# Smaller pieces in the loads, one copy on ScalarE, the mask on another queue, and warm-up matmuls behind the scores

## The chip, the cores and the metric

The kernel runs on one core of a Trainium2 chip. The metric is the time of one execution on the device in microseconds; lower is better.

## The reference

Two layers follow one another. The first is an attention over 8 batches, 8 heads, 576 positions and 64 numbers a head. Its output is the sum of a pooled attention (queries, keys and values averaged over groups of 4) and a local one, in which a position sees those less than 4 away. The second is a mixture of 8 experts: each of the 4,608 tokens goes to the expert with the largest logit, through two matrices with a ReLU between them, and the result is multiplied by the gate's probability.

```python
q_d = q.reshape(B, H, Sd, 4, D).mean(axis=3)      # k_d and v_d alike
out_up = np.repeat(sm_attn(q_d, k_d, v_d), 4, axis=2)
mask = np.abs(pos[:, None] - pos[None, :]) < 4
out_local = softmax(where(mask, scale * q @ k.T, -1e9)) @ v
x = (out_up + out_local)                          # as [4608, 512]
expert = argmax(x @ w_gate, axis=1)
y = probs[expert] * (relu(x @ w1[expert]) @ w2[expert])
```

## The kernel before

**Attention.** 32 passes each take two heads, which lie on the two halves of the 128 partitions. The list `PASS` writes out by hand in which order the steps of a pass are issued; a pair (step, lag) means that in pass i the step works for pass i - lag, so that steps of several passes are interleaved. `s_loc` computes the local scores in 10 blocks of 58 queries and 64 keys: four matmuls first add the mask, 40 more the products. `max_loc`, `sub_loc`, `exp_loc`, `sums`, `eps`, `inv` and `norm` make the softmax on VectorE and ScalarE, `t_loc` and `e_loc` transpose it, and `pv_loc` multiplies it with the values. The pooled attention has the same steps (`s_d`, `max_d`, `exp_d`, `t_d`, `e_d`, `pv_d`); its averages are made by GpSimd in `pool_qk`, `pool_qk2`, `pool_v` and `pool_v2`. `out_d` and `add_up` sum both into `XT`, the input of the second layer.

**Loads.** All loads of a pass are issued on SyncE's queue: `load_qk` (a row of 580 query and 586 key numbers on each of 128 partitions, three buffers), `load_vd` (a row of 1,024 numbers on each of 72 partitions, two buffers), `load_vw` (two buffers) and, from pass 11 on, quarters of the first expert's weights. A load waits until the buffer that it writes is free, and those behind it on the queue wait with it. ScalarE's queue carries the constants at the start: `cb`, the mask and `cf`.

**Routing.** Every four passes 4 or 5 tiles of 128 tokens are complete. The steps `r_mm` to `r_last` compute their expert and their place in that expert's block; the running count per expert is `crun`, which begins as a copy of eight constants after pass 2. `x_rows` turns the tokens back into rows, and `scatter` writes them by an indirect DMA of GpSimd. The state of a routing step lies in the dictionary `RS`.

**Warm-up.** Before and between the first passes `warm` issues matmuls of 128x512 zeros that nobody reads: 9 at the start, then 5, 8 and 5 after passes 0, 1 and 2 (`WARM`).

**Experts.** From about 190 us on `s1`, `s2`, `split_w1` and `split_w2` work through the experts, with float32 split into a high and a low part.

Of the kernel before, what the change touches and what calls it, by code (L numbers as in the profile page):

```python
# [29 lines left out]
KPAD = (NG - 1) * QB + KW  # L30
R = 4
# [12 lines left out]
WARM = (9, 5, 8, 5)  # L44
# [46 lines left out]
def attention_moe_kernel(ctx: ExitStack, tc: tile.TileContext, qk, vw, vd, wg, w1, w2, cst, csb, out):  # L91
# [33 lines left out]
    nc.scalar.dma_start(maskb, csb[:, B_MASK:])  # L125
# [113 lines left out]
    def s_loc(i):  # L239
# [8 lines left out]
        for c in range(NC):  # L248
            for h, t in ((0, 0), (1, 1), (0, 1), (1, 0)):
# [3 lines left out]
                                 x[r, QPAD + g * QB:QPAD + g * QB + KW],  # L253
# [142 lines left out]
    def r_mm(m, tiles):  # L396
        c = tiles[0] * 128
        p = RS[m, "p"] = bank()
# [10 lines left out]
    def r_lg(m, tiles):  # L409
        lg = RS[m, "lg"] = rp.tile([128, 384], F32, name="over", bufs=1)  # L410
        w = 256 if len(tiles) == 4 else 384
        nc.scalar.activation(lg[:, :w], RS[m, "p"][:, :w], AF.Copy)

    def r_turn(m, tiles):
        lg = RS[m, "lg"]
        p = RS[m, "p"] = bank()
# [6 lines left out]
    def r_max(m, tiles):  # L423
        T = len(tiles)
        RS[m, "pl"] = RS[m, "p"][:, :T * 32].rearrange("p (t e) -> p t e", e=32)[:, :, :E]
        RS[m, "m"] = rp.tile([128, 5], F32, name="rm")
        nc.vector.tensor_reduce(RS[m, "m"][:, :T], RS[m, "pl"], axis=AX.X, op=OP.max)

    def r_sub(m, tiles):
        T = len(tiles)  # L430
        d = RS[m, "d"] = RS[m, "p"][:, 256:296].rearrange("p (t e) -> p t e", e=E)
        nc.vector.tensor_sub(d[:, :T], RS[m, "pl"], RS[m, "m"][:, :T, None].to_broadcast([128, T, E]))

    def r_exp(m, tiles):
# [639 lines left out]
```

## Time and profile before

| | |
|---|---|
| median of 3 runs | 647.17 us (645.33 to 647.36) |
| the profiled execution | 644.67 us, its span 642.9 us |
| TensorE, share of the span busy | 96% |
| VectorE | 55% |
| ScalarE | 53% |
| GpSimd | 35% |
| SyncE's DMA queue, share of 16 engines | 49.0% |

The shares are averages over two unlike stages: in the attention passes all engines are busy, in the experts' stage TensorE alone is full. The span runs from the first to the last instruction of the profiled execution; its time also holds the start and the end.

### The profile page before, as it was taken

What the parts mean: (1) busy time and instruction counts of PE and PEld (TensorE: products, weight loads), DVE (VectorE), ACT (ScalarE), POOL (GpSimd) and SP (SyncE); (2) the same over time, 40 slices, a digit from 0 to 9 for tenths busy, and PEclk for the clock granted to TensorE, in tenths of its full rate; (3) what the DMA queues carried; (4) which work ended last, traced back from release to release, by engine and by line L of the source; (5) the groups of instructions that cost most, each with busy time, mean ns of one, the idle gap of its engine ahead of it and who ended that gap; (6) DMA issues with size and microseconds to landing.
All of it is one profiled execution on the core that took longest, in us unless ns stands there. A gap on an engine that the chain in (4) does not pass through costs nothing.

```text
span 642.9 us, 15721 instructions
## 1 busy us (share of the span) xinstructions
PE 617.6 (96%) x6123; PEld 507.9 (79%) x6123; DVE 352.3 (55%) x691; ACT 343.3 (53%) x941; POOL 226.6 (35%) x348
## 2 busy tenths in 40 slices
PE   7899999999979899999999999999999999999994
PEld 4678887787768798888888888888888888888873
DVE  5999988888854573751571174175038166115020
ACT  4899999999964353543452263264235154223120
POOL 7877899999924311111111101101011111110111
PEclk9999999999989999999999999999999999999997
DMA  8998999999862794383274276258137537010001
GB/s 286 286 269 285 292 302 286 292 280 290 239 195 84 187 304 136 122 224 90 84 191 138 66 187 192 68 155 213 56 109 183 181 112 197 35 47 1 34 18 43
DMA packets 68612, 108.65 MB, mean 169 GB/s; under 512 B 15724, under 2 KB 39804, under 8 KB 68496
## 3 DMA queue, kind: packets, MB, share of 16 engines
q1 hardware_dynamic: 62080, 87.78, 49.0%
q0 software_dynamic: 5984, 19.01, 7.9%
q8 instruction: 66, 1.08, 0.8%
q14 instruction: 50, 0.41, 0.2%
q10 hardware_dynamic: 432, 0.37, 0.2%
HBM read 87.09 MB, written 23.67 MB: 172 GB/s over the span
## 4 chain that ended last, share of the span: by engine, by line
PE 68%; issue 10%; POOL 7%; DMA 5%; DVE 5%; ACT 2%; SPq 1%; POOLq 0%; another core or an unknown queue 0%; DVEq 0%; ACTq 0%
PE p L675 8%; PE p L674 8%; PE p L676 8%; PE p L690 7%; PE p L688 7%; PE p L689 7%; POOL xs L550 2%; DMA vd<-in_vd_dram 2%; PE pD L305 2%; POOL vdt L230 2%; PE pX L770 2%; PE pX L789 2%; PE pX L342 1%; PE pS L251 1%; PE pX L329 1%
## 5 line engine op out<-in xcount | busy, mean ns | idle before, releaser
L695 POOL DMA_INDIRECT out_dram<-y,tix x39 | 37.9, 971 | 213.3 <-ACT y L707 201.9
L674 PE MATMUL p<-xh,w1h 128*128 128x512 f32 (+1 forms) x288 | 106.4, 370 | 0.8 <-ACT xh L621 0.7
L675 PE MATMUL p<-xl,w1h 128*128 128x512 f32 (+1 forms) x288 | 105.7, 367 | 0.8 <-DVE xl L622 0.8
L676 PE MATMUL p<-xh,w1l 128*128 128x512 f32 (+1 forms) x288 | 105.5, 366 | 0.0
L688 PE MATMUL p<-w2h,hh 128*128 128x512 f32 x256 | 101.1, 395 | 0.0
L689 PE MATMUL p<-w2l,hh 128*128 128x512 f32 x256 | 99.8, 390 | 0.5 <-DVE w2l L664 0.5
L690 PE MATMUL p<-w2h,hl 128*128 128x512 f32 x256 | 99.9, 390 | 0.0
L679 DVE SCALAR_TENSOR_TENSOR hl<-p,hh 128x512 fp32r<-128x512 f32 (+1 forms) x72 | 45.5, 632 | 94.3 <-ACT hh L678 93.6
L678 ACT ACTIVATE hh<-p 128x512 fp32r<-128x512 f32 (+1 forms) x72 | 39.6, 551 | 78.1 <-PE p L676 75.6
L707 ACT ACTIVATE y<-p,gi 128x512 f32<-128x512 f32 x32 | 22.0, 689 | 91.2 <-PE p L690 86.8
L674 PEld LDWEIGHTS p<-xh,w1h 128*128 128x128 f32 x288 | 54.7, 190 | 10.7 <-ACT xh L621 1.1
L675 PEld LDWEIGHTS p<-xl,w1h 128*128 128x128 f32 x288 | 54.7, 190 | 9.6 <-DVE xl L622 0.9
L676 PEld LDWEIGHTS p<-xh,w1l 128*128 128x128 f32 x288 | 54.6, 190 | 8.7
L689 PEld LDWEIGHTS p<-w2l,hh 128*128 128x128 f32 x256 | 48.1, 188 | 10.6 <-DVE w2l L664 0.9
L690 PEld LDWEIGHTS p<-w2h,hl 128*128 128x128 f32 x256 | 48.1, 188 | 10.2
L688 PEld LDWEIGHTS p<-w2h,hh 128*128 128x128 f32 x256 | 48.1, 188 | 9.5
L664 DVE TENSOR_TENSOR w2l<-raw,w2h 128x512 fp32r<-128x512 f32 x64 | 43.3, 681 | 2.1 <-DMA xs<-xr,ix 1.5
L622 DVE TENSOR_TENSOR xl<-pX,xh 128x512 fp32r<-128x512 f32 x38 | 24.7, 684 | 35.2 <-ACT xh L621 34.2
L194 ACT ACTIVATE w1h<-raw 128x512 fp32r<-128x512 f32 (+1 forms) x72 | 42.1, 584 | 0.0
L550 POOL DMA_INDIRECT xs<-xr,ix x36 | 36.4, 1012 | 15.6 <-ACT xr L525 6.9
L663 ACT ACTIVATE w2h<-raw 128x512 fp32r<-128x512 f32 x64 | 39.8, 626 | 2.8 <-DMA xs<-xr,ix 2.8
L230 POOL TENSOR_TENSOR vdt<-vd 72x512 f32<-72x512 f32 x32 | 40.9, 1279 | 0.3
(152 smaller groups left out, 1240.1 us busy)
## 6 DMA issues: line engine op xcount, KB each, us to landing
raw<-in_w_dram SPq DMA_DIRECT2D x59, 512.0 KB
qk<-in_qk_dram SPq DMA_DIRECT2D x32, 583.0 KB
vw<-in_vw_dram SPq DMA_DIRECT2D x32, 320.0 KB
vd<-in_vd_dram SPq DMA_DIRECT2D x32, 288.0 KB
xrow<-xs SPq DMA_DIRECT2D x32, 192.0 KB
xrow<-xs SPq DMA_DIRECT2D x32, 128.0 KB
xs<-zs SPq DMA_DIRECT2D x6, 512.0 KB
raw<-in_w_dram SPq DMA_DIRECT2D x20, 128.0 KB
```

The source lines that it names most:

```text
L194: nc.scalar.activation(hi[:, s], src[:, s], AF.Copy)
L230: nc.gpsimd.tensor_add(t2, v[:, 0:2], v[:, 2:4])
L550: ins = nc.gpsimd.indirect_dma_start(out=xs, out_offset=bass.IndirectOffsetOnAxis(ap=IDX[m, t], axis=0), in_=xr, in_offset=None)
L663: nc.scalar.activation(hi, src, AF.Copy)
L664: nc.vector.tensor_sub(lo, src, hi)
L674: nc.tensor.matmul(p, wh[:, fs], xh[:, k, r], start=(k == 0), stop=False)
L675: nc.tensor.matmul(p, wh[:, fs], xl[:, k, r], start=False, stop=False)
L676: nc.tensor.matmul(p, wl[:, fs], xh[:, k, r], start=False, stop=(k == 3))
L679: nc.vector.scalar_tensor_tensor(hl[:, f, r], p, 0.0, hh[:, f, r], op0=OP.max, op1=OP.subtract)
L688: nc.tensor.matmul(p, hh, wh, start=(f == 0), stop=False)
L689: nc.tensor.matmul(p, hh, wl, start=False, stop=False)
L690: nc.tensor.matmul(p, hl, wh, start=False, stop=(f == 7))
```

## The change

- `load_qk` and `load_vd` keep their amount, but their rows land in several pieces with a gap of two numbers behind each: the row of queries and keys as two pieces of 586 numbers (six columns of padding are added to the queries), the row of pooled values as four of 256. The host lays the queries out accordingly, and `pool_qk`, `pool_v` and `s_loc` read at the new offsets.
- The mask is loaded on SyncE's queue, behind the first queries.
- The first copy of `crun` is issued on ScalarE instead of VectorE.
- Warm-up: 4 matmuls after pass 0; 7 in pass 2 and 5 in pass 3, each directly behind that pass's `s_loc`; none between passes 1 and 2.
- `RS` gets the first tile into its keys, and `x_rows`, `split_w2` and `s1` are cut into helper functions that are called in the order in which their instructions stood.

```diff
...
 PC = 2 * QB
 QPAD = NG * QB
 KPAD = (NG - 1) * QB + KW
+KOFF = KPAD + 2
 R = 4
 SD = S // R
 DB = 48
...
 NT = N // 128
 NX = 9
 NEG = -8.0e9
-WARM = (9, 5, 8, 5)
+WARM = (9, 4, 7, 5)
 
 C_ID, C_TOK, C_CAP, C_DESC, C_SUM = 0, 128, 164, 172, 180
 C_PAIR = C_SUM + 32
...
     QK, VW, VD, QKD, VDS, A, AD, AT, XT, MXD, SMD, ADT, PS_, PD, PV, IV, QKT, VDT, MX, BX, IVD = ({} for _ in range(21))
 
     def load_qk(i):
-        QK[i] = p1.tile([128, QPAD + KPAD], F32, name="qk", bufs=3)
-        nc.sync.dma_start(QK[i], qk[i])
+        QK[i] = p1.tile([128, 2 * KOFF], F32, name="qk", bufs=3)
+        nc.sync.dma_start(QK[i].rearrange("p (a x) -> p a x", a=2)[:, :, :KPAD], qk[i].rearrange("p (a x) -> p a x", a=2))
 
     load_qk(0)
     cb = consts.tile([128, B_MASK], BF, name="cb")
     nc.scalar.dma_start(cb, csb[:, :B_MASK])
     maskb = p1.tile([128, B_END - B_MASK], BF, name="mask", bufs=1)
-    nc.scalar.dma_start(maskb, csb[:, B_MASK:])
+    nc.sync.dma_start(maskb, csb[:, B_MASK:])
     load_qk(1)
     cf = consts.tile([128, C_END], F32, name="cf")
     nc.scalar.dma_start(cf[:, :C_LIM], cst[:, :C_LIM])
...
     nc.vector.memset(wsrc, 0.0)
     wp = psPV.tile([128, 1024], F32, name="pPV")[:, :512]
 
-    def warm(n, late=False):
-        p = bank() if late else wp
+    def warm(n):
         for _ in range(n):
-            nc.tensor.matmul(p, wsrc[:, :128], wsrc, start=True, stop=True)
+            nc.tensor.matmul(wp, wsrc[:, :128], wsrc, start=True, stop=True)
 
     warm(WARM[0])
     wgt = consts.tile([128, 4, 32], F32, name="wgt")
...
     nc.vector.memset(onesf, 1.0)
 
     def load_vd(i):
-        VD[i] = p1.tile([DC, R, 2, 2, D], F32, name="vd")
-        nc.sync.dma_start(VD[i].rearrange("p r c h d -> p (r c h d)"), vd[i])
+        VD[i] = p1.tile([DC, R, 4 * D + 2], F32, name="vd")
+        nc.sync.dma_start(VD[i][:, :, :4 * D], vd[i].rearrange("p (r x) -> p r x", r=R))
 
     def load_vw(i):
         VW[i] = p2.tile([128, NC, 2, D], F32, name="vw", bufs=2)
...
         x = QK[i]
 
         def sl(r):
-            return bass.AP(tensor=x.tensor, offset=x.offset + r, ap=[x.ap[0], [QPAD + HALO, 2], [R, SD], [2, 2]])
+            return bass.AP(tensor=x.tensor, offset=x.offset + r, ap=[x.ap[0], [KOFF + HALO, 2], [R, SD], [2, 2]])
         t1 = p1.tile([128, 2, SD, 2], F32, name="qkt", bufs=1)
         nc.gpsimd.tensor_add(t1, sl(0), sl(1))
         QKT[i] = t1
...
         nc.gpsimd.tensor_add(QKD[i], t1[:, :, :, 0], t1[:, :, :, 1])
 
     def pool_v(i):
-        v = VD[i]
+        v = VD[i][:, :, :4 * D].rearrange("p r (c h d) -> p r c h d", c=2, h=2)
         t2 = p1.tile([DC, 2, 2, 2, D], F32, name="vdt", bufs=1)
         nc.gpsimd.tensor_add(t2, v[:, 0:2], v[:, 2:4])
         VDT[i] = t2
...
                 g, s, r = 2 * c + t, h ^ t, slice(h * 64, h * 64 + 64)
                 nc.tensor.matmul(p[t * 64:t * 64 + QB, s * 512 + c * KW:s * 512 + (c + 1) * KW],
                                  x[r, g * QB:(g + 1) * QB],
-                                 x[r, QPAD + g * QB:QPAD + g * QB + KW],
+                                 x[r, KOFF + g * QB:KOFF + g * QB + KW],
                                  start=False, stop=(c == NC - 1), skip_group_check=True)
 
     def halves(a):
...
     def r_mm(m, tiles):
         c = tiles[0] * 128
-        p = RS[m, "p"] = bank()
+        p = RS[m, tiles[0], "p"] = bank()
...
-    def x_rows(m, t):
-        p = bank()
+    def x_tr(m, t):
+        p = BX["x", m, t] = bank()
         for k in range(4):
             nc.tensor.transpose(p[:, k * 128:(k + 1) * 128], XT[m][:, k, t * 128:(t + 1) * 128], ident)
+
+    def x_ev(m, t):
+        p = BX.pop(("x", m, t))
         xr = xrs[:, x_slot(m, t)]
         nc.scalar.activation(xr[:, :DM].rearrange("p (b k d) -> p k b d", k=4, d=32),
                              p.rearrange("p (k b d) -> p k b d", k=4, d=32), AF.Copy)
+
+    def x_rows(m, t):
+        x_tr(m, t)
+        x_ev(m, t)
 
     prev_sc = []
 
...
         nc.gpsimd.memset(t, 0.0)
 
     def split_w2(e, f):
+        w2_open(e, f)
+        w2_part(e, f, 0)
+        w2_part(e, f, 1)
+
+    def w2_open(e, f):
         if (e, f) == (0, 0):
             home("tgi", 2)
             home("ttix", 1)
             home("gap", 16)
-        hi, lo = W2[e, f] = tuple(mp[f // 6].tile([128, DM], F32R, name=f"w2{n}{f}") for n in "hl")
+        W2[e, f] = tuple(mp[f // 6].tile([128, DM], F32R, name=f"w2{n}{f}") for n in "hl")
+
+    def w2_part(e, f, n):
+        hi, lo = W2[e, f]
         src = raws[place[2, e, f // 2]][:, (f % 2) * 512:(f % 2) * 512 + 512]
-        nc.scalar.activation(hi, src, AF.Copy)
-        nc.vector.tensor_sub(lo, src, hi)
+        if n == 0:
+            nc.scalar.activation(hi, src, AF.Copy)
+        else:
+            nc.vector.tensor_sub(lo, src, hi)
+
+    HP = {}
 
     def s1(e, f, r=slice(0, FIRST)):
+        for n in range(3):
+            s1_part(e, f, r, n)
+
+    def s1_part(e, f, r, n):
         if e not in HT:
             HT[e] = tuple(mp[0].tile([128, 8, FIRST], F32R, name=f"h{w}") for w in "hl")
-        xh, xl = XH[e, 0]
-        p = h_bank()[:, :r.stop - r.start]
-        fs = slice(f * 128, (f + 1) * 128)
-        for k in range(4):
-            wh, wl = W1[e, k]
-            nc.tensor.matmul(p, wh[:, fs], xh[:, k, r], start=(k == 0), stop=False)
-            nc.tensor.matmul(p, wh[:, fs], xl[:, k, r], start=False, stop=False)
-            nc.tensor.matmul(p, wl[:, fs], xh[:, k, r], start=False, stop=(k == 3))
         hh, hl = HT[e]
-        nc.scalar.activation(hh[:, f, r], p, AF.Relu)
-        nc.vector.scalar_tensor_tensor(hl[:, f, r], p, 0.0, hh[:, f, r], op0=OP.max, op1=OP.subtract)
+        if n == 0:
+            xh, xl = XH[e, 0]
+            p = HP[e, f] = h_bank()[:, :r.stop - r.start]
+            fs = slice(f * 128, (f + 1) * 128)
+            for k in range(4):
+                wh, wl = W1[e, k]
+                nc.tensor.matmul(p, wh[:, fs], xh[:, k, r], start=(k == 0), stop=False)
+                nc.tensor.matmul(p, wh[:, fs], xl[:, k, r], start=False, stop=False)
+                nc.tensor.matmul(p, wl[:, fs], xh[:, k, r], start=False, stop=(k == 3))
+        elif n == 1:
+            nc.scalar.activation(hh[:, f, r], HP[e, f], AF.Relu)
+        else:
+            nc.vector.scalar_tensor_tensor(hl[:, f, r], HP.pop((e, f)), 0.0, hh[:, f, r], op0=OP.max, op1=OP.subtract)
 
     def down(e, hcol, get, between={}):
         p = get()
...
         if 11 <= i < 31:
             raw_part((i - 11) // 4, (i - 11) % 4)
 
+    def keep(i):
+        if 2 <= i < len(WARM):
+            warm(WARM[i])
+
     PASS = (
-        (exp_loc, 1), (rb_turn, 5), (t_d0, 3), (rc_place, 6), (eps, 2), (max_d, 1), (inv, 2), (s_loc, 0),
+        (exp_loc, 1), (rb_turn, 5), (t_d0, 3), (rc_place, 6), (eps, 2), (max_d, 1), (inv, 2), (s_loc, 0), (keep, 0),
         (rb_max, 5), (ld_qk, -2), (pool_qk, -1), (w1_hi, 0), (ld_vd, -1), (inv_d, 2), (rb_sub, 5), (ld_x, 0),
         (pv_loc, 3), (norm, 2), (rb_eps, 6), (e_d1, 3), (rb_top, 5), (rc_rk, 6), (max_scale, 1), (e_d0, 3),
         (max_loc, 0), (norm_d, 2), (ra_mm, 4), (pv_d, 3), (rb_first, 5), (rc_cs, 6), (rb_exp, 5), (pool_v2, 1),
...
     steps(-1)
     for i in range(NP):
         steps(i)
-        if i + 1 < len(WARM):
-            warm(WARM[i + 1], i >= 3)
+        if i == 0:
+            warm(WARM[1])
         if i == 2:
-            nc.vector.tensor_copy(crun, cf[:, C_CAP:C_CAP + E])
+            nc.scalar.copy(crun, cf[:, C_CAP:C_CAP + E])
         if i == 28:
             nc.sync.dma_start(cf[:, C_LIM:], cst[:, C_LIM:])
         if i == 29:
...
 
 
 def _layout(q, k, v):
-    qp = np.zeros((B, H, D, QPAD), q.dtype)
+    qp = np.zeros((B, H, D, KPAD), q.dtype)
     qp[..., :S] = q.transpose(0, 1, 3, 2)
     kp = np.zeros((B, H, D, KPAD), k.dtype)
     kp[..., HALO:HALO + S] = k.transpose(0, 1, 3, 2)
-    qk = np.concatenate([qp.reshape(NP, 128, QPAD), kp.reshape(NP, 128, KPAD)], axis=2)
+    qk = np.concatenate([qp.reshape(NP, 128, KPAD), kp.reshape(NP, 128, KPAD)], axis=2)
     vp = np.zeros((B, H, KPAD, D), v.dtype)
     vp[:, :, HALO:HALO + S] = v
     w = np.stack([vp[:, :, g * QB:g * QB + KW] for g in range(NG)], axis=2)
```

## Rows read from the trace of the kernel before

In the tables of stretches a row gives start and end (us), its length, then for TensorE, its weight loads, VectorE, ScalarE and GpSimd the busy time with the number of instructions, TensorE's granted clock, the DMA share and GB/s. In the orders of time a row gives start, length (us), engine, line, operation, what it writes and reads with shapes, and in brackets the idle time before it and what ended that.

**Rows 1.** Stretches of the attention passes.

```profile
20.00:46.00 26.00, 24.42 (x604) 19.45 (x605) 24.86 (x51) 23.91 (x91) 19.90 (x22) 1.00 0.96 276
46.00:57.00 11.00, 10.89 (x253) 9.28 (x253) 10.63 (x26) 11.00 (x46) 7.46 (x11) 1.00 0.84 246
57.00:110.00 53.00, 52.37 (x1243) 43.10 (x1243) 47.24 (x110) 51.17 (x189) 49.71 (x69) 1.00 0.98 295
```

**Rows 2.** The chain that ended last (start, length, work).

```profile
16.64 2.28 DVE crun L925
```

**Rows 3.** Order of time on VectorE, 14 to 26 us.

```profile
14.23 0.82 DVE L264 TENSOR_REDUCE mx<-pS 128x10 f32<-128x640 f32 x1 [0.44 <-PE pS L251]
...
16.56 2.37 DVE L925 COPY crun<-cf 128x8 f32<-128x8 f32 x1
...
18.84 0.59 DVE L310 TENSOR_REDUCE mxd<-pD 128x3 f32<-128x432 f32 x1
...
20.53 0.82 DVE L264 TENSOR_REDUCE mx<-pS 128x10 f32<-128x640 f32 x1
...
25.28 0.82 DVE L264 TENSOR_REDUCE mx<-pS 128x10 f32<-128x640 f32 x1
```

**Rows 4.** Order of time on GpSimd beside that copy.

```profile
17.75 1.14 POOL L219 TENSOR_TENSOR qkt<-qk 128x576 f32<-128x576 f32 x1
```

**Rows 5.** Order of time on ScalarE, 15 to 20 us.

```profile
15.95 0.74 ACT L271 ACTIVATE A<-A 128x640 f32<-128x640 f32 x1 [0.21 <-DVE A L268]
...
19.47 0.20 ACT L313 ACTIVATE mxd<-mxd 128x3 f32<-128x3 f32 x1 [2.22 <-DVE mxd L310]
```

**Rows 6.** Line 505: count, then min/median/max ns, first and last start.

```profile
L505 ACT COPY xr<-cf x8: 183/216/221, 50.7 to 201.2; 128x4 f32<-128x4 f32 x4, 128x5 f32<-128x5 f32 x4
```

**Rows 7.** Order of time on TensorE, 11 to 24 us.

```profile
11.44 1.90 PE L138 MATMUL pPV<-wsrc 128*128 128x512 bf16 x8
13.27 0.33 PE L245 MATMUL pS<-mask,cb 64*64 64x320 bf16 x4
...
16.43 1.24 PE L138 MATMUL pPV<-wsrc 128*128 128x512 bf16 x5
...
20.02 0.72 PE L370 MATMUL pPV<-ADT,vds 72*64 72x144 f32 x8 [0.65 <-ACT ADT L350]
...
22.11 0.95 PE L305 MATMUL pD<-qkd 64*64 64x144 f32 x12 [0.67 <-ACT AD L319]
...
23.69 0.33 PE L245 MATMUL pS<-mask,cb 64*64 64x320 bf16 x4
```

**Rows 8.** Waits up to 14 us (total, times, longest).

```profile
PE pS L245 <- DMA mask<-in_csb_dram: 1.0, 1, 1.0
```

**Rows 9.** Stretches with loads of 4,096, 2,048 and 512 B.

```profile
372.60:373.50 0.90, 0.90 (x6) 0.74 (x5) 0.90 (x3) 0.55 (x2) 0.00 (x0) 1.00 0.95 385
425.40:426.80 1.40, 1.40 (x8) 1.17 (x7) 0.57 (x2) 0.82 (x2) 0.00 (x0) 1.00 0.99 386
327.00:329.00 2.00, 2.00 (x10) 1.65 (x10) 1.35 (x3) 1.64 (x3) 0.00 (x0) 1.00 1.22 192
```

**Rows 10.** GpSimd's waits, 20 to 57 us (total us, times, longest).

```profile
POOL qkt L219 <- DMA qk<-in_qk_dram: 6.5, 5, 1.8
```

**Rows 11.** Order of time on SyncE's queue, two issues.

```profile
20.37 0.43 SPq L119 DMA_DIRECT2D qk<-in_qk_dram  x1
...
72.90 0.44 SPq L119 DMA_DIRECT2D qk<-in_qk_dram  x1
```

**Rows 12.** Order of time on GpSimd, the uses of these two loads.

```profile
26.39 1.15 POOL L219 TENSOR_TENSOR qkt<-qk 128x576 f32<-128x576 f32 x1 [1.28 <-DMA qk<-in_qk_dram]
...
80.79 1.15 POOL L219 TENSOR_TENSOR qkt<-qk 128x576 f32<-128x576 f32 x1
```

**Rows 13.** GpSimd's groups, 57 to 110 us (busy us, mean ns, idle).

```profile
L230 POOL TENSOR_TENSOR vdt<-vd 72x512 f32<-72x512 f32 x10 | 12.8, 1284 | 0.1
...
L219 POOL TENSOR_TENSOR qkt<-qk 128x576 f32<-128x576 f32 x9 | 10.3, 1148 | 0.0
```

More of the change, by code (lines that the diff above doesn't have):

```diff
@@ L409, in r_lg @@
     def r_lg(m, tiles):
-        lg = RS[m, "lg"] = rp.tile([128, 384], F32, name="over", bufs=1)
+        lg = RS[m, tiles[0], "lg"] = rp.tile([128, 384], F32, name="over", bufs=1)
         w = 256 if len(tiles) == 4 else 384
-        nc.scalar.activation(lg[:, :w], RS[m, "p"][:, :w], AF.Copy)
+        nc.scalar.activation(lg[:, :w], RS[m, tiles[0], "p"][:, :w], AF.Copy)
     def r_turn(m, tiles):
-        lg = RS[m, "lg"]
-        p = RS[m, "p"] = bank()
+        lg = RS[m, tiles[0], "lg"]
+        p = RS[m, tiles[0], "p"] = bank()
         for u in range(2):
@@ L447, in r_first @@
         T = len(tiles)
-        nc.vector.tensor_reduce(RS[m, "m"][:, :T], RS[m, "sc"][:, :T], axis=AX.X, op=OP.max)
+        nc.vector.tensor_reduce(RS[m, tiles[0], "m"][:, :T], RS[m, tiles[0], "sc"][:, :T], axis=AX.X, op=OP.max)
     def r_hot(m, tiles):
         T = len(tiles)
-        oh = RS[m, "oh"] = rp.tile([128, 5, E], BF, name="oh")
-        nc.vector.tensor_tensor(oh[:, :T], RS[m, "sc"][:, :T], RS[m, "m"][:, :T, None].to_broadcast([128, T, E]),
+        oh = RS[m, tiles[0], "oh"] = rp.tile([128, 5, E], BF, name="oh")
+        nc.vector.tensor_tensor(oh[:, :T], RS[m, tiles[0], "sc"][:, :T], RS[m, tiles[0], "m"][:, :T, None].to_broadcast([128, T, E]),
                                 op=OP.is_equal)
@@ L457, in r_gate @@
         T = len(tiles)
-        gt = RS[m, "gt"] = rp.tile([128, 5], F32, name="gt")
-        nc.vector.tensor_reduce(gt[:, :T], RS[m, "ex"][:, :T], axis=AX.X, op=OP.add)
+        gt = RS[m, tiles[0], "gt"] = rp.tile([128, 5], F32, name="gt")
+        nc.vector.tensor_reduce(gt[:, :T], RS[m, tiles[0], "ex"][:, :T], axis=AX.X, op=OP.add)
     def r_eps(m, tiles):
         T = len(tiles)
-        gt = RS[m, "gt"]
+        gt = RS[m, tiles[0], "gt"]
         nc.scalar.activation(gt[:, :T], gt[:, :T], AF.Copy, bias=1e-9)
@@ L477, in r_cs @@
     def r_cs(m, tiles):
-        cs = RS[m, "cs"] = rp.tile([128, E], F32, name="cs")
-        nc.vector.tensor_reduce(cs, RS[m, "oh"][:, :len(tiles)].rearrange("p t e -> p e t"), axis=AX.X, op=OP.add)
+        cs = RS[m, tiles[0], "cs"] = rp.tile([128, E], F32, name="cs")
+        nc.vector.tensor_reduce(cs, RS[m, tiles[0], "oh"][:, :len(tiles)].rearrange("p t e -> p e t"), axis=AX.X, op=OP.add)
     def r_run(m, tiles):
-        nc.gpsimd.tensor_add(crun, crun, RS[m, "cs"])
+        nc.gpsimd.tensor_add(crun, crun, RS[m, tiles[0], "cs"])
     def r_rk(m, tiles):
         T = len(tiles)
-        rk = RS[m, "rk"] = rp.tile([128, 5, E], F32, name="rk", bufs=1)
-        nc.vector.tensor_mul(rk[:, :T], RS[m, "p"][:, :T * E].rearrange("p (t e) -> p t e", e=E), RS[m, "oh"][:, :T])
+        rk = RS[m, tiles[0], "rk"] = rp.tile([128, 5, E], F32, name="rk", bufs=1)
+        nc.vector.tensor_mul(rk[:, :T], RS[m, tiles[0], "p"][:, :T * E].rearrange("p (t e) -> p t e", e=E), RS[m, tiles[0], "oh"][:, :T])
     def r_pos(m, tiles):
         T = len(tiles)
-        pos = RS[m, "pos"] = rp.tile([128, 5], F32, name="pos")
-        nc.vector.tensor_reduce(pos[:, :T], RS[m, "rk"][:, :T], axis=AX.X, op=OP.add)
+        pos = RS[m, tiles[0], "pos"] = rp.tile([128, 5], F32, name="pos")
+        nc.vector.tensor_reduce(pos[:, :T], RS[m, tiles[0], "rk"][:, :T], axis=AX.X, op=OP.add)
     def r_ix(m, tiles):
```

26 lines of the change are left out of this document (13 added, 13 removed).

## The prediction

> **What bounds the kernel now.** I read the table of stages first. From 20 to 110 us the kernel is in its attention passes, and there no engine alone is full: from 20 to 46 us VectorE works 24.86 of 26.00 us, from 57 to 110 us TensorE works 52.37 and GpSimd 49.71 of 53.00 us, and the DMA engines show a share of 0.96 and 0.98 in these two, and 0.84 in the eleven microseconds between [rows 1]. TensorE's granted clock is 1.00 throughout these stretches. Most of the change lies in the first four passes, so I read each engine's order of time there. In the chain that ended last the first copy of the count stands with 2.28 us, on VectorE [rows 2]. So in this stage a wait on VectorE is a delay of everything. Later the chain passes to ScalarE, GpSimd and TensorE, but each of these is reached through the one before it, in program order; a pass that starts earlier on VectorE starts earlier on all of them, as long as the loads come in time. That condition is where the prediction can fail.
>
> **The copy of the count.** The copy of 128x8 numbers takes 2.37 us on VectorE, from 16.56 to 18.93 us. The maximum over 128x640 numbers takes 0.82 us [rows 3], so the length of that row is not work. GpSimd runs an addition from 17.75 to 18.89 us, and the copy ends 0.04 us after that [rows 4]: it looks as if it waited for GpSimd to let go. Without it the next row, the pooled maximum at 18.84 us, starts 2.28 us earlier by the chain's piece, and that is the gain. ScalarE, which waited 2.22 us for that maximum, no longer does [rows 5]. On ScalarE the same kind of copy, 128x4 or 128x5 from the same tile, takes 0.183 to 0.221 us [rows 6]. It is issued between the last eviction of pass 2 and the exponential of pass 3, and there ScalarE is idle 0.21 us for VectorE [rows 5]: cost nothing, and 0.2 us where that gap closes. Behind it on ScalarE stand that exponential and what VectorE sums from it; the matmul that reads the count first is in the routing of pass 9.
>
> **The warm-up matmuls.** After pass 0 four run instead of five. Eight take 1.90 us [rows 7], so one is 0.24 us; the scores of pass 1 stand right behind them on TensorE, so up to 0.24 us comes back. In pass 2 eight stood in front of the scores, which start at 13.27 us; now seven stand behind them. The scores could start 1.8 us earlier, but VectorE is idle only 0.44 us for them before its maximum at 14.23 us [rows 3], so at most 0.44 us of this counts. In pass 3 five, 1.24 us, move from in front of the scores to in front of the local values' matmuls. The work up to the scores of pass 4 keeps its sum: from 16.43 to 23.69 us are 7.26 us, in which TensorE idles 0.65 and 0.67 us for ScalarE [rows 7], which now comes sooner. That leaves 5.94 us and puts the scores of pass 4 at 22.4 us, or at 22.0 us with 0.4 us of what was won before. From their start to the maximum that waits for them pass 2 shows 0.9 us (13.27 to 14.2 us), so they are ready at 22.9 us; VectorE took them up at 25.28 us [rows 3] and, 2.5 to 2.8 us ahead, wants them at 22.5 to 22.8 us. I take 0.5 us of gain from the warm-ups and 0.2 us of loss for this limit; the ends are a gain of 0.7 us and a loss of 0.4 us.
>
> **The mask's queue.** TensorE waits 1.0 us for the mask before the first scores [rows 8]. On the queries' queue it lands behind the first queries. Little of this counts, since the pooled scores, which come next on TensorE, need the queries that GpSimd pools meanwhile. In return the second queries and the first two blocks of values go behind 160 KB, some 0.6 us at the 276 GB/s of the first stretch [rows 1]. GpSimd waits for them, but its results are used passes later. I take nothing; the ends are a gain of 1.0 us, the whole wait, and a loss of 0.6 us.
>
> **The pieces.** A row of queries and keys becomes two pieces of 2,344 B instead of one of 4,664 B, a row of pooled values four of 1,024 B instead of one of 4,096 B. That is 128 and 216 packets more in a pass, 344 in all, 21.5 for each of 16 DMA engines. No row prices these sizes in this stage; I bound them by stretches of the expert stage in which one size is moved. With 4,096 B the rate is 385 GB/s at a share of 0.95, 405 GB/s for full engines; with 2,048 B it is 386 at 0.99, 390 GB/s [rows 9]. For one of 16 engines that is 162 ns for 4,096 B and 168 ns for two pieces: 6 ns for an added packet. With 512 B it is 192 at 1.22, 157 GB/s [rows 9], or 52 ns a piece where the rate of 2,048 B would give 21 ns: 31 ns for a packet. So a pass costs each DMA engine 0.13 us more at the one end and 0.67 us at the other; a gain I can't exclude either, since the new pieces also share the engines with others in another order. I take 0.15 us, near the row of 2,048 B, because 2,344 B is most of the bytes. Six columns of padding add 0.5% to a load, 0.01 us.
>
> The Trainium skill speaks against this edit: by "DMA: Bandwidth & Descriptors", in the section on why small descriptors are slow, a packet carries about three cycles over its 32-byte beats. At the beat of the 4,096 B rows (1.3 ns) that would be an estimate of 4 ns a packet, 0.08 us a pass instead of my 0.13 us; the trace agrees in direction, with 6 ns.
>
> Is it hidden? It is while queries land before GpSimd asks. From 20 to 57 us GpSimd waits for them five times, 6.5 us in all [rows 10], but with slack behind it. A load that was waited for took 6.0 us from issue to use (20.37 to 26.39 us); the shortest from 57 to 110 us is 7.9 us (72.90 to 80.79 us), and there GpSimd idles 0.0 us for them [rows 11 to 13]. So 1.9 us or less of cover is left, less because the DMA share is higher there. With 0.15 us a pass over the ten passes of that stretch 1.5 us is used up, and nothing is lost. The edits to the routing's keys and to the split helper functions issue the same instructions in the same order and cost nothing.
>
> **Sum.** 2.28 + 0.5 - 0.2 = 2.58 us of gain, say 2.5. The profiled execution took 644.67 us, 642.9 of them in the span; that becomes 642.2. The median of the runs is 647.17 us, 2.5 above the profiled execution, so I forecast 644.7. The runs lie up to 2.0 us apart; a change within 0.3% (1.94 us) can't be told from none.
>
> **Rivals.** *The DMA engines take the gain back.* If all passes come 2.5 us earlier, the same bytes have to land in less time. By the shares the DMA engines are idle 1.0 us of 20 to 46, 1.8 us of 46 to 57 and 1.1 us of 57 to 110 us [rows 1]: 3.9 us in all. For it speaks that GpSimd already waits for queries before 57 us; against it the 7.9 us above. If half of the idle time can't be filled, and the pieces take 1.5 us of the cover, the gain shrinks to about 0.6: 646.6 us.
>
> *The smaller pieces make the kernel slower.* From 20 to 110 us there are some eighteen passes (ten additions of values from 57 us on [rows 13], and eight before at 4.75 us each, the distance of the maxima at 20.53 and 25.28 us [rows 3]). At 31 ns a packet they cost 12.1 us of DMA time; 3.9 us of idle time and 1.9 us of cover take part of it, 6.3 us shows as GpSimd waiting for queries, less 2.5: 3.8 us slower, 651.0 us. It decides from (2.5 + 1.94 + 3.9 + 1.9) / 18 = 0.57 us a pass on, or 26 ns a packet. For it speaks the row of 512 B, against it that of 2,048 B.
>
> *GpSimd's addition of the values gets cheaper.* It takes 1.284 us for 72x512 numbers, while the addition of the queries takes 1.148 us for more, 128x576 [rows 13]. One difference is that the two operands of the former lie 2,048 B apart; with the two new columns they lie 2,064 B apart. At the rate of the other it would take 1.02 us, 0.26 us less in each of ten passes in which GpSimd has no idle time: 2.6 us on top, 642.1 us. Nothing shows that distance is the cause.
>
> **How the numbers follow.** The gain arrives (2.0 to 3.2 us): 0.40. With cheaper additions: 0.12. Taken back in part or whole (0 to 1.9 us): 0.31. Pieces slow the loads: 0.17, of which 0.14 by more than 0.3%. Hence faster 0.52, same 0.34, slower 0.14. The range goes from 641.0 (cheaper additions, and 1 us for the runs' spread) to 649.2, which leaves out the upper part of the slow case; the likeliest case alone has 643.9 to 645.2.
>
> **What would show it.** The maximum of pass 3 right behind the sums, no copy on VectorE, the scores of pass 4 near 22 us, and GpSimd's first scatter of routed rows earlier by 2.5 us. Waits of GpSimd for queries between 57 and 110 us would show the first two rivals, more than 6.5 us of them before 57 us the start of it; an addition of values near 1.0 us the third. I am wrong if VectorE finds another wait at 16 us, if TensorE's granted clock falls below 1.00 in one of these stretches, or if the 2.5 us are there at 46 us and gone at 110 us.

## The result and the profile of the changed kernel

The changed kernel took 655.5 us (median of 4 runs, 654.41 to 656.58) against 647.26 us (4 runs of the kernel before, 645.33 to 648.45): ratio 1.0132, 95% interval 1.0106 to 1.0158. The forecast was 644.7 us. The profiled execution took 654.67 us with a span of 652.9 us, 10.0 us more than before.

The stretches that answer to [rows 1], and the one ahead of them:

```profile
10.00:20.00 10.00, 7.53 (x125) 5.14 (x126) 6.83 (x11) 5.70 (x23) 8.98 (x10) 0.83 0.85 231
20.00:46.00 26.00, 23.15 (x568) 17.97 (x569) 20.91 (x42) 20.67 (x79) 19.61 (x22) 0.93 0.98 268
46.00:57.00 11.00, 9.63 (x216) 8.03 (x214) 10.36 (x29) 10.20 (x41) 6.70 (x10) 1.00 0.92 258
57.00:110.00 53.00, 51.48 (x1179) 42.59 (x1180) 44.38 (x102) 47.51 (x176) 43.91 (x61) 0.97 0.92 259
```

VectorE has lost 3.95 us of work between 20 and 46 us and GpSimd 5.8 us between 57 and 110 us, so these engines now stand still where they were the pace. The granted clock, 1.00 in all of [rows 1], is 0.93 and 0.97 in two of these stretches and 0.83 from 10 to 20 us. What stands still first is read from the waits. TensorE's, up to 110 us (total, times, longest):

```profile
PE pS L251 <- issue: 2.6, 1, 2.6
PE pPV L357 <- issue: 2.5, 1, 2.5
PE pD L305 <- POOL qkd L225: 1.9, 2, 1.3
...
PE pS L251 <- DMA qk<-in_qk_dram: 1.2, 2, 0.8
```

"Issue" is time in which the engine waited for nothing that the profile shows. In two places TensorE stands 2.5 us and more in the middle of a step. In order of time the first one reads:

```profile
27.35 0.72 PE L370 MATMUL pPV<-ADT,vds 72*64 72x144 f32 x8
...
30.44 0.72 PE L251 MATMUL pS<-qk 64*58 64x64 f32 x37
33.76 0.32 PE L251 MATMUL pS<-qk 64*58 64x64 f32 x3 [2.59 <-issue]
...
34.62 1.20 PE L370 MATMUL pPV<-ADT,vds 72*64 72x144 f32 x8
```

37 of the 40 products of a pass's scores are done, all 40 read the same buffer, and the last three come 2.59 us later. Behind the stop the same eight matmuls take 1.20 us instead of 0.72. The stretches around the first stop and behind the second show why:

```profile
31.00:34.70 3.70, 1.11 (x54) 0.91 (x49) 1.48 (x4) 2.24 (x10) 2.99 (x4) 1.00 1.03 342
34.70:38.10 3.40, 3.40 (x23) 2.66 (x25) 2.52 (x5) 1.76 (x4) 1.48 (x2) 0.50 1.07 215
58.60:62.00 3.40, 3.40 (x30) 2.70 (x21) 0.83 (x2) 1.24 (x3) 3.34 (x4) 0.50 0.69 197
```

The clock falls to 0.50 (1.2 of 2.4 GHz) for 3.4 us each time. Both stops lie on the chain that ended last, which between 20 and 62 us runs through TensorE alone:

```profile
31.16 2.59 issue
...
55.63 2.51 issue
```

They are also where the time is lost. VectorE's maximum of the local scores (`max_loc`) starts in pass 3 0.7 us later than in the trace of before, in pass 6 5.5 us, in pass 9 5.3 us, in pass 10 9.6 us and in the last pass 11.1 us later: 4.8 us are lost across the first stop and 4.3 us across the second.

What TensorE lacked are its own instructions. The trace has a DMA queue of kind "instruction", q8, whose 66 transfers move 1.08 MB, 16 KB each; in the passes there is one for about every 128 weight loads of TensorE. The following is worked out from the transfers' records: when a block began to move, and in brackets how many weight loads TensorE had begun since the last multiple of 128.

```
before   18.9 (22)  26.4 (43)  31.6 (37)   36.5 (28)  41.0 (26)  46.2 (22)  50.8 (19)
changed  24.1 (52)  31.2 (102) 36.1 (30)   41.8 (22)  47.8 (41)  55.7 (109) 60.6 (23)
```

No block that starts 19 to 52 weight loads behind the multiple has a stop behind it in these two rows (in other traces stops of 0.5 us and more follow blocks from 36 on). The two at 102 and 109 are the two stops, and each stop ends about 2.5 us after its block began to move: 33.76 us after 31.2, 58.15 us after 55.7. In all twenty traces of this document TensorE has 86 stops for instructions of 0.5 us or more between 20 and 175 us, and every one ends 2.2 to 3.2 us after a block began to move. So TensorE has run dry and waits for its next block. That the block in turn waits for the DMA engines, which the loads keep busy (share 1.03 in that stretch), is argued and not seen. By the Trainium skill ("Runtime: NRT & Kernel Launch", section on instruction fetch mechanics) an engine brings in its next 16 KiB block by a DMA queue of its own while it runs the present one, and this is mostly hidden. The trace agrees for the kernel before (0.6 us of such waits up to 110 us), not for this one (5.4 us).

The steps of the prediction that can be read here. VectorE and ScalarE around the count, which answer to [rows 3] and [rows 5]:

```profile
16.87 0.81 DVE L274 TENSOR_REDUCE smd<-A 128x10 f32<-128x640 f32 x1
19.52 0.61 DVE L310 TENSOR_REDUCE mxd<-pD 128x3 f32<-128x432 f32 x1 [1.84 <-PE pD L305]
```

```profile
18.98 0.19 ACT L955 COPY crun<-cf 128x8 f32<-128x8 f32 x1
```

The copy takes 0.19 us and is off VectorE, but VectorE now waits 1.84 us for the pooled scores at the same place. TensorE and GpSimd at that time, which answer to [rows 7] and [rows 4], show where this comes from:

```profile
12.09 0.83 PE L305 MATMUL pD<-qkd 64*64 64x144 f32 x10 [1.26 <-POOL qkd L225]
...
14.02 1.20 PE L251 MATMUL pS<-qk 64*58 64x64 f32 x40 [0.84 <-DMA qk<-in_qk_dram]
15.55 2.49 PE L138 MATMUL pPV<-wsrc 128*128 128x512 bf16 x6 [0.33 <-PE pS L251]
```

```profile
10.14 1.15 POOL L219 TENSOR_TENSOR qkt<-qk 128x576 f32<-128x576 f32 x1 [2.67 <-DMA qk<-in_qk_dram]
```

The loads are late. SyncE's queue at the start:

```profile
1.51 0.57 SPq L126 DMA_DIRECT2D mask<-in_csb_dram  x1
2.12 0.57 SPq L120 DMA_DIRECT2D qk<-in_qk_dram  x1
2.74 0.96 SPq L207 DMA_DIRECT2D vd<-in_vd_dram  x1
3.75 0.56 SPq L120 DMA_DIRECT2D qk<-in_qk_dram  x1
```

The third queries are issued at 3.75 us (2.19 us in the trace of before), behind the mask and behind longer issues: 0.96 us for values in four pieces, 0.57 us for queries in two, where whole rows of queries take 0.43 [rows 11]. The scores of pass 2 wait for them, the clock falls to 0.50 from 14.2 to 17.6 us, and six warm-up matmuls take 2.49 us. GpSimd waits for queries between 20 and 57 us and between 57 and 110 us [rows 10]:

```profile
POOL qkt L219 <- DMA qk<-in_qk_dram: 8.7, 7, 2.2
...
POOL qkt L219 <- DMA qk<-in_qk_dram: 5.4, 4, 3.1
```

Its addition of values [rows 13] is no cheaper:

```profile
L230 POOL TENSOR_TENSOR vdt<-vd 72x512 f32<-72x512 f32 x9 | 11.6, 1286 | 0.2
```

### The profile page after: what moved, and what is told of

It reads as the page before. It is cut to its first block, busy times and chain, and to the rows that moved or that the text cites. A ratio compares the mean times of both kernels' runs of the same rounds, so it can differ in the third digit from the quotient of the medians.

```text
span 652.9 us, 15716 instructions
## 1 busy us (share of the span) xinstructions
PE 622.7 (95%) x6118; PEld 512.0 (78%) x6121; DVE 350.3 (54%) x690; ACT 344.5 (53%) x942; POOL 226.8 (35%) x348
## 3 DMA queue, kind: packets, MB, share of 16 engines
q8 instruction: 66, 1.08, 0.7%
## 4 chain that ended last, share of the span: by engine, by line
PE 80%; issue 8%; DMA 4%; ACT 3%; DVE 1%; POOL 1%; SPq 1%; another core or an unknown queue 0%; POOLq 0%; DVEq 0%; ACTq 0%
PE p L700 8%; PE p L699 8%; PE p L701 8%; PE p L716 7%; PE p L714 7%; PE p L715 7%; PE pD L305 4%; PE pX L329 3%; PE pPV L370 3%; PE pX L342 3%; PE pPV L357 3%; PE pS L251 3%; PE pX L523 2%; PE pX L796 2%; PE pX L815 2%
## 5 line engine op out<-in xcount | busy, mean ns | idle before, releaser
L699 PEld LDWEIGHTS p<-xh,w1h 128*128 128x128 f32 x288 | 54.4, 189 | 10.2 <-ACT xh L628 1.1
L715 PEld LDWEIGHTS p<-w2l,hh 128*128 128x128 f32 x256 | 48.1, 188 | 10.2 <-DVE w2l L681 0.5
L219 POOL TENSOR_TENSOR qkt<-qk 128x576 f32<-128x576 f32 x32 | 36.7, 1146 | 19.9 <-DMA qk<-in_qk_dram 19.9
```

What stands on the lines that cost most here:

```text
L699: nc.tensor.matmul(p, wh[:, fs], xh[:, k, r], start=(k == 0), stop=False)
L715: nc.tensor.matmul(p, hh, wl, start=False, stop=False)
```

## The experiments

Each ratio is to the kernel before on the same chip, with its 95% interval. Three theories stand in the expectations; the first four call them A, B and C. *Late instructions*: added transfers make TensorE's instruction blocks late. *Lost lead*: the mask ahead of the queries and the other warm-ups make the start late, and GpSimd never gets it back. *Longer issue*: the pieces lengthen SyncE's issues, the time that its queue needs to send a load off. "Waits for instructions" are the rows of TensorE's waits that end in "issue", summed up to 110 us of one execution: 0.6 us in the trace of before, 5.4 us in the changed kernel's.

**One half each.** `e1_pieces` has only the pieces, `e2_rest` only the mask, the count and the warm-ups.

> Before, with the pieces of both loads alone. Theory A (the smaller pieces make TensorE wait for its own instructions: two idle stretches of about 2.7 us inside a step, each followed by 3.4 us at half clock): 6 to 9 us slower, with at least one such stretch before 80 us. Theory B (the start is late: mask ahead of the second queries, other warm-ups, so that GpSimd loses 3 us of lead): within 2 us of before, GpSimd's second addition of queries near 7.0 us. Theory C (longer issue on SyncE's queue, 0.8 instead of 0.3 us for the values): 1 to 4 us slower, without idle stretches on TensorE.

> Before, with the count on ScalarE, the mask on the queries' queue and the new warm-ups, rows in one piece. Theory A: 1 to 3 us faster, because the copy's 2.3 us come back. Theory B: 4 to 9 us slower, with GpSimd's second addition of queries near 10 us instead of 7.0 us. Theory C: within 2 us of before.

Measured: 1.0026 (0.999 to 1.0062), waits for instructions 6.2 us, and 1.0022 (0.9977 to 1.0067), 4.0 us. Neither half makes up the change, and neither can be told from none. Late instructions expected 6 to 9 us for the pieces and a gain for the rest; 1.7 and 1.4 us of loss were measured, and behind stops of up to 2.0 us the clock stayed 1.00. The lost lead expected GpSimd's second addition of queries near 7.0 and 10 us; it starts at 8.8 and 8.6 us. The longer issue has both times right, but wanted no idle stretches on TensorE.

**Each kind of piece.** `e3_qk_pieces` and `e4_vd_pieces`.

> Before, with two pieces for a row of queries and keys alone. Theory A: part of the pieces' loss, 2 to 5 us, if the number of pieces decides (128 of 344 packets more in a pass). Theory B: within 2 us. Theory C: under 1 us, since the issue of this load grows from 0.43 to 0.55 us only.

> Before, with four pieces for a row of pooled values alone. Theory A: 3 to 7 us slower (216 of 344 packets more in a pass), with idle stretches of over 2 us on TensorE. Theory B: within 2 us. Theory C: 1 to 4 us slower, since the issue of this load grows from 0.32 to 0.82 us. A cheaper addition of values (near 1.0 us) would show here as well.

Measured: 1.0037 (1.0012 to 1.0062), 6.8 us, and 1.0056 (1.0019 to 1.0093), 2.8 us. Each costs something by itself; the stops of over 2 us that were expected for the values are not in that trace (longest 1.1 us), and the longer issue wanted under 1 us for the queries and keys, where 2.4 us (0.8 to 4.0) were measured.

**The kernel before, and all four edits without the helper functions.**

> The kernel before, unchanged, beside the others on this chip: ratio 1.000. It is run for its trace. In the four runs before it, each with only one part of the change, all traces lose 2 to 4 us between 80 and 100 us, also the one without pieces. If the kernel before loses them here too, they belong to the chip and not to a part.

> All four edits at once on the kernel before, without the helper functions and the routing's keys. If those cost nothing, the ratio is that of the change, 1.013 (1.0106 to 1.0158). If the parts only add (0.26% for the pieces, 0.22% for the rest), it is 1.005, and the other 0.8% belong to the first comparison alone. Theory of the late instructions: two or more stalls of over 2 us in which TensorE waits for its own instructions before 60 us, each followed by 3.4 us at half clock. Theory of the lost lead: GpSimd's third addition of queries starts 3 us or more after that of the kernel before.

Measured: 0.9997 (0.9969 to 1.0025), 1.4 us, and 1.0086 (1.0056 to 1.0115), 7.6 us with two stops of over 2.5 us. One of them ends at 32.8 us, the other only at 89.6 us, so the two or more before 60 us did not come. GpSimd's third addition of queries starts at 12.8 us against 11.8 us in `e0_before`, not 3 us later. Between 80 and 100 us the kernel before loses 0.7 us against its first trace (on another chip than the first four runs, of which the pieces alone lose 3.4 us there), and the count alone, below, 1.3 us on theirs; so most of that loss does not belong to a chip.

**The change less one edit.** `e9_no_mask` leaves the mask on ScalarE's queue, `e10_no_warm` keeps the old warm-ups.

> The change with the mask left on ScalarE's queue. Theory of the lost lead: the second queries are issued 0.6 us earlier and meet 160 KB less ahead of them; GpSimd's third addition of queries gets 1 us or more back, and the time falls by 1 to 3 us against all four edits. Theory of the late instructions: as many packets as with all four, so the same number of stalls and the same time within 1 us.

> The change with the warm-up matmuls as before (9, 5, 8, 5 in front of the scores). If the half clock at 14 us comes from the missing matmuls between passes 1 and 2, the granted clock stays 1.00 from 10 to 20 us and the time falls by 1 to 2 us against all four edits. Theory of the late instructions: the stalls behind 25 us stay, and with them most of the loss. Theory of the lost lead: GpSimd's third addition starts as late as with all four, and the time is the same within 1 us.

Measured: 1.0065 (1.0028 to 1.0101) and 1.0058 (1.0026 to 1.009), both with a stop of 1.9 us or more in the scores near 30 us. With the old warm-ups the clock is 1.00 from 10 to 20 us, as expected, and most of the loss stays. The two ratios lie 0.2% and 0.3% below that of all four edits, which the intervals can't tell from none. GpSimd's third addition gets nothing back: it starts at 13.4 and 13.6 us instead of 12.8. That speaks against the lost lead as the main cause, and so does the changed kernel's own trace, in which the maximum of pass 3 starts at 21.2 us, between the 20.5 and 21.9 us of the two traces of before.

**The count alone and the warm-ups alone.**

```diff
-            nc.vector.tensor_copy(crun, cf[:, C_CAP:C_CAP + E])
+            nc.scalar.copy(crun, cf[:, C_CAP:C_CAP + E])
```

> Only the copy of the count moves to ScalarE. By the prediction's working the 2.28 us on VectorE come back: 0.9965. Theory of the late instructions: nothing in this edit adds packets, so TensorE's waits for its own instructions stay near the 2.4 to 2.6 us of the kernel before and the gain stands. Rival, the DMA engines take the gain back: GpSimd's additions of queries from the sixth on start as before, and the ratio is 1.000.

> Only the warm-up matmuls move. By the prediction's working 0.3 us of gain, 0.9995. If earlier scores make TensorE ask for instructions earlier, in the stretch in which the loads fill the DMA engines, then a stall of over 1 us appears near 30 us and the ratio is 1.002 or more, as for all edits but the pieces (1.0022).

Measured: 1.0000 (0.9973 to 1.0027), 3.3 us, and 1.0041 (1.0009 to 1.0074), 3.7 us. Both expectations of the prediction's working missed. For the count the theory of the late instructions missed too, as it let the gain stand; the rival had the ratio right. In the count's trace the copy's time is won and given back in two places. The first is VectorE's next maximum, here in the count's trace and then in that of the kernel before (`e0_before`):

```profile
20.98 0.82 DVE L264 TENSOR_REDUCE mx<-pS 128x10 f32<-128x640 f32 x1 [0.85 <-PE pS L251]
```

```profile
21.92 0.82 DVE L264 TENSOR_REDUCE mx<-pS 128x10 f32<-128x640 f32 x1
```

The pooled maximum that stood behind the copy starts at 18.34 instead of 20.23 us, 1.89 us earlier; 0.42 us of that this trace was ahead already, so the copy brings 1.47 us. The scores of pass 3 stand behind the old warm-ups on TensorE and are only 0.42 us earlier (20.18 instead of 20.60 us). So VectorE waits 0.85 us for them, and of the 1.47 us 0.52 are left. The second place is a stop of TensorE, in order of time:

```profile
29.05 0.72 PE L251 MATMUL pS<-qk 64*58 64x64 f32 x35
31.16 0.33 PE L251 MATMUL pS<-qk 64*58 64x64 f32 x5 [1.39 <-issue]
```

The kernel before has the same stop at the same matmul, shorter and later (trace of `e0_before`):

```profile
29.98 0.72 PE L251 MATMUL pS<-qk 64*58 64x64 f32 x35
31.24 0.33 PE L251 MATMUL pS<-qk 64*58 64x64 f32 x5 [0.54 <-issue]
```

The scores start 0.93 us earlier, and their last five matmuls only 0.08 us earlier. The blocks began to move at 28.5 and 28.8 us, so both stops end 2.5 to 2.7 us behind that. In the warm-ups' trace the stop is one step later and costs more, since the clock falls for 6.8 us (stretches of the stop and behind it):

```profile
35.20:37.60 2.40, 0.18 (x13) 0.09 (x8) 2.37 (x4) 1.86 (x9) 1.27 (x2) 1.00 0.90 285
38.20:45.00 6.80, 6.80 (x86) 5.30 (x87) 2.51 (x6) 3.88 (x12) 5.25 (x6) 0.50 0.82 248
```

**Where the pieces are made, and a dose.** `e11_memory_gap` puts the gap in the source, so that the rows in the buffers stay whole; `e12_more_pieces` makes 4 and 8 pieces in the same way.

```diff
-        nc.sync.dma_start(QK[i], qk[i])
+        nc.sync.dma_start(QK[i].rearrange("p (a x) -> p a x", a=2), qk[i].rearrange("p (a x) -> p a x", a=2)[:, :, :583])
...
```

> The same pieces made by a gap in the source instead of the destination: 2 and 4 a row, 2,332 and 1,024 bytes, while the rows in the buffers stay whole and every other instruction reads as before. If the packets cost the time, the ratio is that of the smaller pieces, 1.003 (0.999 to 1.006), and TensorE waits 7 to 9 us for its own instructions up to 175 us. If the place in the buffers costs it (GpSimd's and TensorE's reads at the new offsets), the ratio is 1.000 and the waits stay at 2.5 us.

> A dose: 4 pieces of 1,168 bytes and 8 of 512 bytes a row, 888 packets more in a pass instead of 344, no other edit. Theory of the late instructions: 6 us more of TensorE's waits for instructions at 344 packets give 15 us at 888, and 1.2% to 2.5% of time. Theory of the lost lead by longer issues: SyncE's issues grow again by half a microsecond each, GpSimd waits for queries over 25 us up to 110 us, and TensorE's own waits stay at 8 us. If the packets only use up idle time of the DMA engines, the ratio is 1.003 as with 344.

Measured: 1.0041 (1.002 to 1.0063), 5.2 us and 6.7 us up to 175 us, and 1.0179 (1.0137 to 1.0221), 7.0 us and 12.2 us up to 175 us. So the pieces themselves cost the time and not the place in the buffers, and the cost grows with them. More packets come with longer issues on SyncE's queue here, and the two were not separated; against the issues stand GpSimd's waits for queries, 17.3 us in the dose where that theory wanted over 25. TensorE's waits of the dose, up to 110 us:

```profile
PE pPV L357 <- issue: 5.1, 4, 2.0
...
PE pS L251 <- issue: 1.1, 1, 1.1
...
PE pD L305 <- issue: 0.8, 2, 0.6
```

The price of a packet can be estimated from the stretch of 20 to 46 us, here the kernel before (`e0_before`) and then the dose:

```profile
20.00:46.00 26.00, 24.44 (x600) 19.28 (x598) 24.45 (x50) 23.33 (x87) 17.81 (x21) 1.00 0.95 272
```

```profile
20.00:46.00 26.00, 22.72 (x530) 17.75 (x518) 20.25 (x38) 20.32 (x77) 18.27 (x20) 0.87 1.00 258
```

272 GB/s at a share of 0.95 are 286 for full engines, against 258. For the 1,191 KB of a pass that is 4.26 and 4.73 us, 0.46 us for 888 packets, 55.5 on each engine: 8 ns a packet. The same division gives 286 to 300 GB/s in the other traces with whole rows and no added bytes, so 8 to 12 ns is the estimate that the traces allow.

**The change again, and the mask alone.**

> The change itself once more, beside the kernel before on one chip. If the helper functions and keys cost nothing it agrees with all four edits on the kernel before, 1.0086 (1.0056 to 1.0115); if they cost something it stays at 1.013. By the theory of the late instructions it shows 8 us or more of TensorE's waits for its own instructions up to 175 us.

> Only the mask's load moves to SyncE's queue. Sum of the parts: 0.9% for all less 0.3% for the pieces and 0.4% for the warm-ups leaves 1.002 for the mask. Theory of the lost lead: GpSimd's second addition of queries starts 0.6 us or more later, 1.001 to 1.003. By the prediction's working 1.000.

Measured: 1.010 (1.0064 to 1.0135), 4.1 us, and 0.9987 (0.996 to 1.0014), 2.6 us. The change as given lies between the first comparison and `e8_all`, so whether the helper functions cost anything is not decided. For the mask the prediction's 1.000 fits; GpSimd's second addition of queries starts at 7.7 us (8.0 in `e0_before`), no later. The 8 us of waits up to 175 us that were expected were 6.2.

**Transfer time taken out and put in.** `e16_count_zs` is the count's copy with the two writes that clear `zs` moved to the last pass; `e17_more_bytes` adds a load that nobody reads in passes 1 to 10.

```diff
...
+        if 1 <= i < 11:
+            extra = p1.tile([32, 1024], F32, name="extra", bufs=2)
+            nc.sync.dma_start(extra, vd[i][:32, :])
```

> The count's copy on ScalarE, and the two writes that clear zs (257 KB, issued in passes 9 and 10) go to the last pass. If full DMA engines took back what the copy gave, 257 KB less before 60 us give 0.9 us at the 272 GB/s of that stretch, 0.9985 with the copy alone at 1.000. If the copy's gain was lost to something else, 1.000.

> The kernel before, with a load of 32 rows of 4,096 bytes (128 KB, which nobody reads) more in each of passes 1 to 10. At the 272 GB/s of 20 to 46 us that is 0.48 us of full DMA engines a pass, 4.8 us in all. If the DMA engines set the pace there, 1.005 to 1.0075, with TensorE's waits for instructions over 4 us or GpSimd's waits for queries over 16 us. If only small pieces delay the instructions, 1.000 to 1.002, and the waits stay at 2.5 and 13 us.

Measured: 0.9986 (0.9958 to 1.0014), 2.4 us: the size that was expected, but not told from none. And 1.0153 (1.0115 to 1.0191), 7.3 us, GpSimd's waits for queries 27.6 us: more than any theory gave. The extra load had waits of its own on SyncE's queue, so it was repeated.

**The dose of bytes repeated, and three edits that add no transfers.** `e19_bytes_wide` loads `[128, 256]` with ten buffers; `e18_count_mask_zs` is the count, the mask and `zs`, with whole rows and the old warm-ups.

> The change's two edits that add no transfer time, the count's copy on ScalarE and the mask on SyncE's queue, with zs cleared in the last pass; rows stay whole, warm-ups as before. If the two small gains add, 0.997 and an interval below 1. If the DMA engines take both back, 0.9985 to 1.000 with an interval that holds 1.

> Again 128 KB more in each of passes 1 to 10, now on 128 partitions in pieces of 1,024 bytes and with ten buffers, so that no load waits for them. Transfer time alone: 0.48 us a pass at 272 GB/s, 4.8 us, 1.005 to 1.0075. If the price of 1.015 came from the wait on SyncE's queue, it falls to that; if it stays at 1.012 or more, full DMA engines charge twice their own time, through TensorE's waits for instructions and half clock.

Measured: 1.0024 (0.9992 to 1.0056), 5.8 us, and 1.004 (1.0012 to 1.0068), 6.0 us. 4.8 us of added transfer time cost 2.6 us (0.8 to 4.4), so full DMA engines do not charge twice; whether the two buffers or the 32 partitions made the first dose dear was not separated. `e18` is not a better version; 1.0024 lies above both of its expectations, though the interval holds 1. Its trace shows the mechanism best: up to pass 13 its maxima stand 0.5 us ahead of the trace of before, then its chain reads

```profile
74.89 0.26 PE pS L245 x4
75.14 0.56 PE pS L251 x37
75.70 0.22 PE pPV L357 x9
75.92 1.68 issue
77.60 0.68 PE pPV L357 x27
78.29 0.65 PE pPV L370 x8
78.94 1.18 PE pX L329 x5
```

The block began to move at 74.9 us, and from 79.0 to 82.4 us the clock is 0.50. By pass 16 the maxima are 5.7 us behind. In the trace of before GpSimd had hardly any idle time here [rows 13] and was the chain; here it looks as if the stop empties that pipeline.

## Why the prediction was wrong

**What bounds the kernel: the step that failed.** I wrote that a pass that starts earlier on VectorE starts earlier on all engines, "as long as the loads come in time", and looked for lateness only in the queries that GpSimd waits for. That step failed, and the runs show two other waits in its place. With the count alone nothing else changed; VectorE won 1.47 us, gave back 0.95 us at scores that stand behind the warm-ups on TensorE, and the rest at a stop of TensorE for its own instructions. In the changed kernel it is these stops, with the half clock behind them, that cost the time. The loads share the DMA engines with TensorE's instruction blocks, and I had counted only the loads among what can be late. This is near the rival in which the DMA engines take the gain back, but by another wait than the one that I watched, and it turned the gain into a loss, which that rival did not.

**The count's copy.** Its local part held: 0.19 to 0.21 us on ScalarE, nothing lost there. The reading that the copy waits for GpSimd held as well: in all eleven traces with the copy on VectorE it ends 0.02 to 0.09 us after one of GpSimd's additions. By the Trainium skill ("SBUF — State Buffer", section on who interferes with whom) VectorE and GpSimd take turns at a shared pair of ports while ScalarE has its own; the trace agrees, since the copy at 18.98 us takes 0.19 us beside an addition of GpSimd. But for that very reason 2.28 us was no fixed price. In the traces of the kernel before the copy takes 2.37 and 1.75 us, with the pieces alone 0.70 and 0.89 us (`e1` and `e11`), with the mask alone 0.86 us, and with the warm-ups alone

```profile
18.39 0.40 DVE L929 COPY crun<-cf 128x8 f32<-128x8 f32 x1
```

So beside the other edits there was much less to win than the sum took from one execution. Its term, 2.28 us of gain, was 0.0 by itself (interval 1.7 us of gain to 1.7 us of loss).

**The warm-ups.** 0.3 us of gain was 2.7 us of loss (0.6 to 4.8). The 0.44 us and the limit at the scores of pass 4 were worked out rightly for a start that keeps its order; a stop of TensorE for instructions, 2.22 us in the trace with the warm-ups alone, was not in the sum; that it comes because TensorE reaches its next block earlier is argued. In the changed kernel the scores of pass 4 start at 26.0 us instead of near 22.

**The mask.** I took nothing; 0.9987 (0.996 to 1.0014) agrees. But "its results are used passes later" does not hold beside the longer issues of the pieces: TensorE waits 1.26 us for the queries that GpSimd pools.

**The pieces.** The price of a packet was about right: 8 to 12 ns by the dose, near the 6 ns taken and far from 31. The cover was the error. The 0.15 us a pass were to go into 1.9 us of cover that the queries had, and nothing was to be lost. With the pieces alone TensorE waits 6.2 us (`e1`) and 5.2 us (`e11`) for instructions up to 110 us, and 1.7 us (0.6 of gain to 4.0) and 2.7 us (1.3 to 4.1) are lost. The issues on SyncE, which grew by 0.13 and 0.49 us, were not priced at all. The rival that the pieces make the kernel slower had the right sign and not the right mechanism: it needed 26 ns a packet. GpSimd does wait 5.4 us for queries between 57 and 110 us, as it wanted, but over most of that stretch, from pass 10 to pass 19, the maxima fall no further behind the trace of before.

**The cheaper addition of values** is refuted: 1,286 ns against 1,284.

**The sum.** Against the 647 us of before, the parts alone make +1.7 or +2.7 (pieces, `e1` or `e11`), +2.7 (warm-ups), 0.0 (count) and -0.8 us (mask), 3.6 to 4.6 us; together they measured 5.6, 6.5 and 8.5 us in three comparisons. Each part has an interval of about 2 us on either side, so it stays open whether the parts add or help one another. Of the 10.0 us in the two traces, 4.8 us are the longer waits for instructions up to 110 us, and three stretches of 3.4 us at half clock cost up to 5.1 us more. The same reckoning holds for all twenty traces. From the maximum of pass 3 to that of pass 31 the trace of before takes 152.3 us, with 2.2 us of waits for instructions in it; the changed kernel's takes 162.8 us, with 8.5 us of waits and 6.8 us at half clock, and the dose's 168.1 us, with 13.2 and 10.2 us. A straight line through the twenty gives 1.0 us of length for each microsecond of waits plus half of the time at half clock (correlation 0.93); farthest from it is `e17`, 5 us above.

Of the signs that were to show me wrong two came in the changed kernel: VectorE finds another wait where the copy stood, 1.84 us, and the granted clock falls below 1.00. The third, a lead that is there at 46 us and gone at 110, shows only in `e18`. The sign of the first two rivals came too, 8.7 and 5.4 us of GpSimd's waits for queries before and behind 57 us.

**Open.** The trace shows when a block starts to move, not when it was asked for; that full DMA engines hold it back is argued from the doses and the shares, not seen. Behind the seven longest stops, 2.2 to 2.7 us, the block began between 0.3 us before and 0.2 us after TensorE stood still, so it can't be excluded that it was asked for only then. `e18` shows that a kernel without added transfers can be hit too, and a profile is one execution, so the waits of one trace and a ratio of many runs agree only loosely: `e4` is slower with 2.8 us, `e18` not measurably with 5.8 us. The granted clock over the whole span was 0.981 in the profiled execution of the changed kernel and 0.985 to 0.987 in its other three, so half clock cost those less.

## What to carry to other kernels

Where the DMA engines show a share near 1.0, a stall that is removed upstream is not a gain until it has been followed to the first engine that then runs dry, and TensorE's own instruction blocks are one of the transfers that can come late: look for "issue" in the middle of a step and for the clock behind it. Smaller pieces cost little each, but they lengthen the issue, and a load's lead is not the only cover that they use up. A wait that depends on what another engine does at that moment is no fixed price: here the same copy took 0.33 to 2.37 us. An edit of 2 us in a pipeline in which one stop with the half clock behind it costs 4 to 5 us has to be timed in many runs.

## What the runs showed of the hardware

A stop of TensorE for instructions of 1.7 to 2.6 us was followed, within 1.4 us of its end, by 3.4 or 6.8 us at a granted clock of 0.50 in the traces of the changed kernel, `e7` and `e18`. Behind the stops of 0.54 and 1.39 us shown above, behind stops of 2.0 us in `e1` and `e3` and behind one of 2.7 us in `e8`, the clock stayed 1.00. In twenty traces TensorE went on 2.2 to 3.2 us after a block of its instructions began to move, behind each of 86 stops of 0.5 us or more. VectorE's copy of 128x8 numbers took 0.33 to 2.37 us and ended 0.02 to 0.09 us after an addition of GpSimd in eleven traces; on ScalarE it took 0.19 to 0.21 us. SyncE's issue of a load with the same bytes took 0.33 us for 72 pieces and 0.82 us for 288, and 0.37 to 0.43 us for 128 pieces and 0.56 us for 256, whether the gap lay in the buffer or in the source. The distance between the two operands of GpSimd's addition, 2,048 or 2,064 bytes, made no difference.
